# Loading the first rows in two column blocks, one transfer for batch 1 and the rest of the first queries, and a rewritten end of the token loop

## The chip, the core and the metric

The kernel runs on one NeuronCore of one Trainium2 chip. The metric is the device time of one execution in microseconds (us); less is better. Three runs of the kernel before took 171.71 to 171.78 us, median 171.75 us. TensorE (PE) multiplies, VectorE (DVE), ScalarE (ACT) and GpSimd (POOL) work on elements, and SyncE (SP) issues nearly all transfers, which 16 DMA engines carry out.

## The reference, cut to what matters

Linear attention over 8 batches of 8 heads, 576 tokens and 64 channels, an RMS norm per head, and then a soft mixture of experts over all 4608 tokens with 32 slots, four for each of eight experts:

```
kv  = einsum('bhsd,bhse->bhde', k, v)
out = einsum('bhsd,bhde->bhse', q, kv)
x   = out / sqrt(mean(out*out, -1) + 1e-6) * g_norm      # -> (4608, 512)
logits = x @ phi                                          # (4608, 32)
d = exp(logits - logits.max(0)); d /= d.sum(0)            # over tokens
slot_input = d.T @ x                                      # 32 slots x 512
slot_out[e] = relu(slot_input[e] @ w1[e]) @ w2[e]         # 8 experts
c = exp(logits - logits.max(1)); c /= c.sum(1)            # over slots
result = c @ slot_out                                     # (4608, 512)
```

All of it is float32. q, k and v are 28.3 MB together, the expert weights 33.6 MB, the result 9.4 MB.

## The kernel before, in words

The 4608 tokens are 36 tiles of 128. The program is written as one list of operations in the order of the Python code; each engine executes its own operations in that order, and `Order.emit` adds a semaphore wait wherever an operand was last written or read by another engine or by a transfer.

Start. SP issues five loads without any wait: `first_in` (phi, the norm's weights and the first half of batch 0's k and v, 9792 bytes a row, 128 rows), `kv0_in` (the rest of batch 0 and half of the first queries), `kv_in[0]` (batch 1's k and v), `q0_in` (the rest of the first queries) and `kv2_in`. TensorE meanwhile multiplies constants (`fill`, `fill_wide`), then forms batch 0's kv matrices in two halves. Later loads go into one arena in SBUF whose places are used again: each waits for the last reader of its place, mostly a matmul.

Token loop. For each tile T, `products(T)` makes one PSUM tile with the attention output and the unscaled logits per head, ACT squares it (`square`) and copies it out (`evict`). Two tiles are a stage: DVE sums the squares (`mean_square`), ACT makes the root by Ln and Exp (`root`), DVE improves it (`newton`), POOL scales (`scale_part`, `scale_x`), DVE adds the heads (`logits`). `kv_step(b, i)` forms the next batch's kv matrices; for batch 1 this stands ahead of tile 3's products. Six tiles are a group: `group_max` takes the running maximum of the logits, `group_max_T` and `group_max_row` bring it to all slots, `group_diag` and `group_exp_PE` broadcast it, `group_exp` takes exponentials and `group_sum` accumulates the slot inputs.

End of the loop (tiles A = 34 and Z = 35). Each of the two is a stage by itself (`STAGES` ends in 1, 1): root, newton, scaling of the logit part (`scale_o`, straight from PSUM), then `logits`, first for A, then for Z. Then `group_max` over the last six tiles, four small matmuls, the row maximum, `group_diag`, a matmul, `group_exp`, `scale_o` of the attention outputs, `group_sum`.

Experts and output. `expert_h(e)` needs w1 and the slot inputs, `expert_y(e, half)` needs w2; both weights stream through the arena, each load behind the last reader of its place. `gather` and `mix` bring the expert outputs to all partitions, `output` makes chunks of the result that go out in stores from SP (a few from POOL); the last store holds a third of the result.

Of the kernel before, what the change touches and what calls it, by code (L numbers as in the profile page):

```python
# [61 lines left out]
SHARED = (5, 11)  # L62
BEHIND = {4: (2, 3), 5: (4, 5, 6, 7)}
HEAD = 144
SCRATCH = 1024
WORK = {
    "kvT": (1, 256), "sq": (2, 1024), "part": (3, 512), "ms": (3, 16), "r0": (2, 16), "r": (3, 16), "r1": (2, 16),
    "top": (1, 128), "diag": (1, 32), "d": (2, 192), "alpha": (2, 1), "cm": (2, 13), "cs": (2, 13),
}
EPS_RMS = 1e-6  # L70
EPS_SUM = 1e-9
# [214 lines left out]
        at += n * size  # L286


def soft_moe_linear_attention(nc, first_in, kv0_in, kv_in, q0_in, kv2_in, kv4_in, kv5_in, t3_in, w_in, out):


    const = Const(nc)
# [12 lines left out]
    def load_row(at, src):  # L305
        nc.sync.dma_start(place(at, src.shape[-1]), src)
# [85 lines left out]
    def pos(T):  # L392
        return T + T // GROUPS[0] + 1
# [115 lines left out]
        nc.scalar.copy(xts[T % NX][:, :, :128], o[:, :, 32:160])  # L509


    def mean_square(s):
        mss[s] = wk.tile([P, STAGES[s] * H], F32, tag="ms", name=f"ms{s}", bufs=3)
        nc.vector.tensor_reduce(
            out=mss[s], in_=sqs.pop(s).rearrange("p t j (w d) -> p (t j w) d", w=2), axis=AX.X, op=ALU.add
        )

    def root(s, home=None):
# [26 lines left out]
                op=ALU.mult,  # L545
            )

    def scale_o(T, o, of_x):

        s = stage_of[T]  # L550
        r = rs_of[s][:, T - starts[s]].rearrange("p (j w) -> p j w", w=2).unsqueeze(3)
        if of_x:
            out = xts[T % NX][:, :, :128].rearrange("p j (w d) -> p j w d", w=2)
            src = o[:, :, 32:160].rearrange("p j (w d) -> p j w d", w=2)
        else:
            parts[s] = wk.tile([P, STAGES[s], H, NS], F32, tag="part", name=f"part{s}", bufs=3)
            out = parts[s][:, T - starts[s]].rearrange("p (j w) n -> p j w n", w=2)
            src = o[:, :, :192].rearrange("p j (c n) -> p j c n", n=NS)[:, :, 0::5]
        nc.vector.tensor_tensor(out=out, in0=src, in1=r.to_broadcast([P, 4, 2, D if of_x else NS]), op=ALU.mult)

    def scale_part(s, engine):
        part = parts[s]
        engine.tensor_tensor(
            out=part, in0=part, in1=rs_of[s].unsqueeze(3).to_broadcast([P, STAGES[s], H, NS]), op=ALU.mult
        )
# [15 lines left out]
        )  # L581


    ds, alphas, held, sums, pbs, pms, tops = {}, {}, {}, {}, {}, {}, {}
    g0 = [sum(GROUPS[:G]) for G in range(len(GROUPS) + 1)]

    def group_max(G):
        at = pos(g0[G])
        nc.vector.tensor_reduce(
            out=L[:, at + GROUPS[G]],  # L590
            in_=L[:, at - (G > 0) : at + GROUPS[G]].rearrange("p t n -> p n t"),
            axis=AX.X,
            op=ALU.max,
        )
        if G < len(GROUPS) - 1:
            tops[G] = wk.tile([P, 4, NS], F32, tag="top", name=f"top{G}", bufs=1)
            nc.vector.tensor_copy(
                out=tops[G], in_=L[:, at + GROUPS[G]].unsqueeze(1).to_broadcast([P, 4, NS])
            )

    def group_max_T(G):
        pm = ps.tile([P, P], F32, tag="m", name=f"pm{G}")
        if G in tops:
            nc.tensor.transpose(pm, tops.pop(G).rearrange("p a n -> p (a n)"), ident)
        for j in range(4 if G == len(GROUPS) - 1 else 0):
            nc.tensor.matmul(
                pm[32 * j : 32 * j + 32], lhsT=L[:, pos(g0[G]) + GROUPS[G]], rhs=ident, start=True, stop=True
            )
        pms[G] = pm

    def group_max_row(G):
        nc.vector.tensor_reduce(out=run_max[G % 2], in_=pms.pop(G), axis=AX.X, op=ALU.max)

    def group_diag(G):
        diag = wk.tile([P, NS], F32, tag="diag", name=f"diag{G}", bufs=1)
        nc.scalar.activation(diag, ident[:, :NS], AF.Copy, scale=run_max[G % 2])
        held[G] = diag

    def group_exp_PE(G):
        pbs[G] = ps.tile([P, NS], F32, tag="m", name=f"pb{G}")  # L620
# [94 lines left out]
    for g in range(2):  # L715
# [7 lines left out]
    load_row(KV_AT[3], kv_in[1])  # L723
    load_row(Q_AT[1] + 8, kv4_in)
    load_row(Q_AT[2], kv5_in)
    T_at, diag_at, pb_at, d_at, sums_at = {}, {}, {}, {}, {}
    for T in range(NT - 2):
        for b in range(1, B):
            for at in kv_steps.get((b, T - first[b]), ()):
                kv_step(b, at)  # L730
        late = [b for b in (1, 2) if T == first[b] - 1]
        o = products(T, (lambda: kv_step(late[0], 2)) if late else None)
        s = ends.get(T - 1)
        if s is not None:
            root(s)
        if T in diag_at:
            group_diag(diag_at[T])
        square(T, o)
        G = d_at.get(T)
        if G is not None:  # L740
            group_exp(G)
            sums_at[T + 1] = G
        evict(T, o)
        if T in T_at:
            group_max_T(T_at[T])
            diag_at[T + 1] = pb_at[T + 2] = T_at[T]
# [24 lines left out]
    tail_ps = ps.tile([P, 2, 512], F32, tag="kv", name="tail")  # L771
    A, Z = NT - 2, NT - 1
    oA = products(A)
    group_diag(G - 1)
    group_exp_PE(G - 1)
    root(s - 2)
    square(A, oA)
    newton(s - 2)
    scale_part(s - 2, nc.gpsimd)
    logits_adds(s - 2)  # L780
    scale_x(s - 2)
# [19 lines left out]
    fill_wide(ps.tile([P, 512], F32, tag="m", name="fill"), LATE_FILL[0])  # L801
    group_max_T(G)
    group_max_row(G)
    group_diag(G)
    scale_o(A, oA, True)
    fill(LATE_FILL[1], home=tail_ps[:, 1], cols=512)
    group_exp_PE(G)
    group_exp(G)
    scale_o(Z, oZ, True)
    fill(LATE_FILL[2], home=tail_ps[:, 1], cols=512)  # L810
    for i in range(0, GROUPS[G], 2):
        group_sum(G, i)
    fill(LATE_FILL[3], home=tail_ps[:, 1], cols=512)


    sTe = wk.tile([P, NE * 4 * NS], F32, tag="sq", name="sTe")
# [9 lines left out]
    fill(LATE_FILL[4], home=tail_ps[:, 1], cols=512)  # L826
    mine = psT[:, :P].rearrange("p (j e k) -> p e j k", j=4, k=SPE)
    last = NE - 1
    nc.vector.tensor_scalar_mul(
# [196 lines left out]
def build_program():  # L1026
    import concourse.bacc as bacc

    nc = bacc.Bacc("TRN2", target_bir_lowering=False, num_devices=1, dynamic_dma_scratch_size=SCRATCH)
    shapes = {  # L1030
        "first": (P, HEAD + 2304), "kv0": (P, 2304 + 2048), "kv": (2, P, TOK), "q0": (P, 2560),
        "kv2": (P, TOK + 2048),
        "kv4": (P, 2560 + TOK), "kv5": (P, 2 * TOK), "t3": (P, 3 * TOK),
        "w": (1, 2 * NE * P * UNIT),
    }
# [68 lines left out]
```

## Time and profile before

| | |
|---|---|
| median of three runs | 171.75 us |
| profiled execution: its time, its span | 171.73 us, 170.4 us |
| PE, DVE, ACT, POOL busy | 151.0, 86.9, 88.5, 59.6 us |
| moved by the DMA engines | 71.65 MB, mean 421 GB/s |
| time of the packets of SP's queue, as a share of 16 engines' span | 97.8% |

The span runs from the first to the last instruction; 1.3 us of the execution's time lie around it. In windows and slices, a DMA share of 1.00 means that the packets of that stretch fill all 16 engines; a packet is counted where it starts, so short stretches can show more than 1. "Idle before" in square brackets is the time that the engine stood idle ahead of a group, with what ended it.

### The profile page before, as it was taken

The page shows a single profiled execution, that of the slowest core. Times are in us where ns is not written, and L with a number is a line of the kernel's source. Part 1 is how long each engine was busy: PE and PEld are TensorE (multiplying, and loading weights), DVE is VectorE, ACT ScalarE, POOL GpSimd, SP SyncE. Part 2 cuts the span into 40 slices and gives each one's busy share as a digit, 9 for nine tenths or more (in the row PEclk, how much of TensorE's full clock was granted, in tenths as well). Part 3 has the DMA queues.
Part 4 walks back from the last instruction along what each step waited for, and adds up shares of the span by engine and source line. Part 5 has one row for each costly group of instructions (what it writes and reads, how often), then busy time and mean ns, then how long its engine had stood idle before and what let it go on. Part 6 is the DMA issues. An engine that isn't in the chain of part 4 may idle for free.

```text
span 170.4 us, 4234 instructions
## 1 busy us (share of the span) xinstructions
PE 151.0 (89%) x1834; PEld 104.0 (61%) x1834; DVE 86.9 (51%) x185; ACT 88.5 (52%) x230; POOL 59.6 (35%) x73
## 2 busy tenths in 40 slices
PE   7998998999999899999899989989999989989200
PEld 3457987979688888796696664345566533454000
DVE  1111437743677265763936798724888036319300
ACT  3015778786965887768849864202234044418300
POOL 7000247757356755366482589300000004000000
PEclk9999999999999999999999999999999999999855
DMA  5999999999999999999999999999999999999996
GB/s 193 440 435 417 478 413 409 457 430 478 419 415 439 432 441 413 419 400 460 400 458 408 448 408 423 431 458 396 431 427 431 452 435 396 427 415 439 415 447 288
DMA packets 3933, 71.65 MB, mean 421 GB/s; under 512 B 742, under 2 KB 742, under 8 KB 874
## 3 DMA queue, kind: packets, MB, share of 16 engines
q1 hardware_dynamic: 3562, 71.18, 97.8%
q8 instruction: 14, 0.23, 0.5%
q0 software_dynamic: 352, 0.20, 0.4%
q14 instruction: 5, 0.04, 0.1%
HBM read 61.94 MB, written 9.44 MB: 419 GB/s over the span
## 4 chain that ended last, share of the span: by engine, by line
PE 54%; DMA 16%; ACT 15%; DVE 6%; issue 1%; SPq 0%
PE psum L215 54%; DMA arena<-in_w_dram 10%; DMA arena<-in_kv_dram 6%; ACT bd L215 4%; ACT sq L215 4%; ACT xall L215 2%; DVE ms L215 2%; DVE logits L215 1%; ACT part L215 1%; ACT arena L215 1%; ACT r L215 1%; ACT d L215 1%; DVE part L215 1%; DVE acc L215 1%; DVE r L215 0%
## 5 line engine op out<-in xcount | busy, mean ns | idle before, releaser
L215 PE MATMUL psum<-bd,arena 128*128 128x192 f32 (+1 forms) x320 | 56.6, 336 | 2.4 <-ACT bd L215 1.2
L215 PEld LDWEIGHTS psum<-bd,arena 128*128 128x128 f32 (+1 forms) x320 | 45.5, 179 | 9.7 <-ACT xall L215 3.5
L215 DVE TENSOR_REDUCE ms<-sq 128x16 f32<-128x1024 f32 (+1 forms) x19 | 22.1, 1162 | 28.6 <-ACT sq L215 28.5
L215 POOL TENSOR_TENSOR part<-part,r 128x512 f32<-128x512 f32 x17 | 17.8, 1047 | 48.9 <-DVE r L215 48.9
L215 POOL TENSOR_TENSOR xall<-xall,r 128x512 f32<-128x512 f32 x34 | 34.7, 1042 | 0.0
L215 ACT ACTIVATE sq<-psum 128x512 f32<-128x512 f32 x36 | 21.5, 596 | 9.0 <-PE psum L215 8.9
L215 PEld LDWEIGHTS psum<-arena 128*64 128x64 f32 (+1 forms) x640 | 18.8, 137 | 6.6 <-issue 3.0
L215 PE MATMUL psum<-arena 128*64 128x64 f32 (+1 forms) x640 | 21.4, 226 | 0.3 <-DMA arena<-in_kv_dram 0.3
L215 ACT COPY xall<-psum 128x512 f32<-128x512 f32 x34 | 20.7, 608 | 0.0
L215 ACT COPY part<-psum 128x256 f32<-128x256 f32 (+1 forms) x38 | 13.7, 359 | 9.2 <-DVE part L215 8.0
L215 DVE TENSOR_REDUCE logits<-part 128x64 f32<-128x512 f32 (+1 forms) x18 | 17.8, 991 | 0.0
L215 PE MATMUL psum<-arena,xall 128*32 128x256 f32 x256 | 15.0, 380 | 0.4 <-DMA arena<-in_w_dram 0.4
L215 DVE COPY arena<-psum 128x768 f32<-128x768 f32 (+1 forms) x12 | 10.5, 889 | 6.8 <-PE psum L215 6.8
L215 ACT COPY arena<-psum 128x768 f32<-128x768 f32 (+1 forms) x14 | 10.2, 754 | 7.1 <-PE psum L215 7.1
L215 PE MATMUL psum<-logits,part 32*128 32x384 f32 x96 | 12.7, 527 | 0.6 <-ACT arena L215 0.4
L215 POOL DMA_DIRECT2D out_dram<-arena x2 | 1.2, 589 | 33.8 <-DVE arena L215 33.8
L215 PE MATMUL psum<-arena,sq 128*32 128x256 f32 x224 | 12.7, 379 | 0.2 <-DVE sq L215 0.2
L215 PEld LDWEIGHTS psum<-arena,xall 128*32 128x32 f32 x256 | 8.1, 110 | 6.9 <-issue 1.4
L215 PE MATMUL psum<-xall,d 128*32 128x258 f32 x144 | 10.8, 390 | 1.0 <-ACT d L215 1.0
L215 ACT COPY bd<-psum 64x128 f32<-64x128 f32 (+1 forms) x32 | 9.8, 308 | 2.4 <-PE psum L215 2.2
L215 PEld LDWEIGHTS psum<-arena,sq 128*32 128x32 f32 x224 | 7.2, 110 | 5.1 <-DVE sq L215 0.5
L215 ACT COPY kvT<-psum 128x256 f32<-128x256 f32 (+1 forms) x9 | 3.1, 348 | 12.6 <-PE psum L215 12.5
(80 smaller groups left out, 129.7 us busy)
## 6 DMA issues: line engine op xcount, KB each, us to landing
arena<-in_w_dram SPq DMA_DIRECT2D x4, 4096.0 KB, 23.8
arena<-in_w_dram SPq DMA_DIRECT2D x4, 2048.0 KB, 20.5
arena<-in_t_dram SPq DMA_DIRECT2D x1, 6912.0 KB, 35.6
arena<-in_w_dram SPq DMA_DIRECT2D x2, 3072.0 KB, 22.9
arena<-in_kv_dram SPq DMA_DIRECT2D x2, 2304.0 KB, 19.0
arena<-in_kv_dram SPq DMA_DIRECT2D x1, 4608.0 KB, 40.3
arena<-in_kv_dram SPq DMA_DIRECT2D x1, 3584.0 KB, 29.9
arena<-in_kv_dram SPq DMA_DIRECT2D x1, 3328.0 KB, 26.0
```

What stands on the lines that cost most here:

```text
L215: inst = getattr(engine, method)(*args, **kwargs)
```

## The change

Four edits.

1. The load of `first_in` is two loads: its first 512 columns (2048 bytes a row) and its other 1936 columns (7744 bytes a row).
2. `q0_in` and `kv_in[0]` are one load, `kv1_in`, 28672 bytes a row. The two parts are neighbours in the arena. The number of loads and the bytes stay as they were.
3. Tiles 34 and 35 are one stage. Both products stand next to each other; one root, one newton and one `logits` serve both. The last group's maximum is taken in steps: over its first two tiles early (`group_max(G, 2)`), the rest by three small operations (`last_max`). ACT scales tile A's attention output in eight pieces (`x_of_o`). There are 7 constant fills where there were 12.
4. `group_diag` and the matmul on it are replaced, in every group, by one transpose of the maximum's broadcast column.

```diff
-STAGES = (2,) * 17 + (1, 1)
+STAGES = (2,) * 18
-LATE_FILL = (4, 3, 3, 1, 1)
+LATE_FILL = (2, 1, 1, 1, 1, 1)
+AHEAD = 512
-    nc.sync.dma_start(arena[:, : HEAD + 2304], first_in)
+    nc.sync.dma_start(arena[:, :AHEAD], first_in)
+    nc.sync.dma_start(arena[:, AHEAD : HEAD + 2304], second_in)
     load_row(KV_AT[0] + 9, kv0_in)
-    load_row(KV_AT[1], kv_in[0])
-    load_row(Q_AT[0] + 8, q0_in)
+    load_row(Q_AT[0] + 8, kv1_in)
     load_row(KV_AT[2], kv2_in)
...
+    def last_max(G):
+        at = pos(g0[G])
+        so_far = L[:, at + GROUPS[G]]
+        m = wk.tile([P, 2, NS], F32, tag="kvT", name="last_max")
+        nc.vector.tensor_tensor(out=m, in0=L[:, at + 2 : at + 4], in1=L[:, at + 4 : at + 6], op=ALU.max)
+        nc.vector.tensor_tensor(out=so_far, in0=so_far, in1=m[:, 0], op=ALU.max)
+        group_top(G, so_far, m[:, 1])
...
-    def group_diag(G):
-        diag = wk.tile([P, NS], F32, tag="diag", name=f"diag{G}", bufs=1)
-        nc.scalar.activation(diag, ident[:, :NS], AF.Copy, scale=run_max[G % 2])
-        held[G] = diag
     def group_exp_PE(G):
-        nc.tensor.matmul(pbs[G], lhsT=ones, rhs=held[G], start=True, stop=True)
+        nc.tensor.transpose(pb, run_max[G % 2].to_broadcast([P, P]), ident)
...
-    mean_square(s - 1)
-    oZ = products(Z)
-    root(s - 1, tail_ps[:, 0, 256 : 256 + H])
-    square(Z, oZ)
-    newton(s - 1)
-    scale_o(A, oA, False)
-    mean_square(s)
-    root(s, tail_ps[:, 0, 256 + H : 256 + 2 * H])
-    logits(s - 1)
+    mean_square(s, slice(0, 1))
+    oZ = products(Z)
+    square(Z, oZ)
+    fill_wide(tail_ps[:, 1], LATE_FILL[0])
+    mean_square(s, slice(1, 2))
+    root(s, tail_ps[:, 0, 256 : 256 + 2 * H])
+    group_exp(G - 1)
+    todo_sums += [(G - 1, i) for i in range(0, GROUPS[G - 1], 2)]
+    group_max(G, 2)
     newton(s)
-    scale_o(Z, oZ, False)
+    scale_o(A, oA)
+    scale_o(Z, oZ)
+    x_of_o(A, oA, True)
     logits(s)
-    group_max(G)
+    last_max(G)
```

On SP, the first five loads of the kernel before and of the changed kernel, with partitions and columns of four bytes:

```order
L215 DMA arena<-in_first_dram 128x2448
L215 DMA arena<-in_kv_dram 128x4352
L215 DMA arena<-in_kv_dram 128x4608
L215 DMA arena<-in_q_dram 128x2560
L215 DMA arena<-in_kv_dram 128x6656
```

```order
L216 DMA arena<-in_first_dram 128x512
L216 DMA arena<-in_second_dram 128x1936
L216 DMA arena<-in_kv_dram 128x4352
L216 DMA arena<-in_kv_dram 128x7168
L216 DMA arena<-in_kv_dram 128x6656
```

Batch 1's k and v were the third load and end now with the fourth; everything from the fifth load on is the same.

On TensorE, ahead of tile 3: the last products of tile 2 (`psum<-bd,arena`), then batch 1's kv matrices (`psum<-arena`), which wait for a load (`dma_2` is batch 1's load before, `dma_3` the second part of the first queries before and the joint load now), then tile 3, and with `64x192` tile 4; before, then now:

```order
L215 MATMUL psum<-bd,arena 128x192 x3
L215 MATMUL psum<-arena 64x64 [waits dma_2]
L215 MATMUL psum<-arena 64x64 x39
L215 MATMUL psum<-bd,arena 128x192 [waits done_scalar]
L215 MATMUL psum<-bd,arena 128x192
L215 MATMUL psum<-ident,kvT 128x128 [waits done_scalar]
L215 MATMUL psum<-ident,kvT 128x128
L215 MATMUL psum<-gphi,kvT 128x128 x2
L215 MATMUL psum<-bd,arena 128x192 x2
L215 MATMUL psum<-bd,arena 64x192 [waits dma_3]
```

```order
L216 MATMUL psum<-bd,arena 128x192 x3
L216 MATMUL psum<-arena 64x64 [waits dma_3]
L216 MATMUL psum<-arena 64x64 x39
L216 MATMUL psum<-bd,arena 128x192 [waits done_scalar]
L216 MATMUL psum<-bd,arena 128x192
L216 MATMUL psum<-ident,kvT 128x128 [waits done_scalar]
L216 MATMUL psum<-ident,kvT 128x128
L216 MATMUL psum<-gphi,kvT 128x128 x2
L216 MATMUL psum<-bd,arena 128x192 x2
L216 MATMUL psum<-bd,arena 64x192
```

The wait for the second part of the first queries has moved ahead, from tile 4 to batch 1's kv matrices before tile 3.

On DVE, the end of the token loop, from the mean squares of tile 34 to the last row maximum (`small<-psum`); before, then now:

```order
L215 SCALAR_TENSOR_TENSOR r<-ms,psum 128x8 [waits done_scalar]
L215 SCALAR_TENSOR_TENSOR r<-r,psum 128x8 [waits done_vector] x2
L215 TENSOR_TENSOR part<-psum,r 128x256 [waits done_vector]
L215 TENSOR_REDUCE ms<-sq 128x8 [waits done_scalar]
L215 TENSOR_REDUCE logits<-part 128x32 [waits done_vector]
L215 SCALAR_TENSOR_TENSOR r<-ms,psum 128x8 [waits done_scalar]
L215 SCALAR_TENSOR_TENSOR r<-r,psum 128x8 [waits done_vector]
L215 SCALAR_TENSOR_TENSOR r<-r,psum 128x8 [waits done_gpsimd,done_vector]
L215 TENSOR_TENSOR part<-psum,r 128x256 [waits done_vector]
L215 TENSOR_REDUCE logits<-part 128x32 [waits done_vector]
L215 TENSOR_REDUCE logits<-logits 128x32 [waits done_gpsimd,done_vector]
L215 SCALAR_TENSOR_TENSOR acc<-acc,alpha,psum 128x258 [waits done_tensor]
```

```order
L216 TENSOR_REDUCE ms<-sq 128x8 [waits done_scalar] x2
L216 TENSOR_TENSOR d<-logits,psum 128x192
L216 TENSOR_REDUCE logits<-logits 128x32
L216 SCALAR_TENSOR_TENSOR r<-ms,psum 128x16 [waits done_scalar]
L216 SCALAR_TENSOR_TENSOR r<-r,psum 128x16 [waits done_vector] x2
L216 TENSOR_TENSOR part<-psum,r 128x256 [waits done_vector]
L216 TENSOR_TENSOR part<-psum,r 128x256
L216 TENSOR_REDUCE logits<-part 128x64 [waits done_vector]
L216 TENSOR_TENSOR kvT<-logits 128x64 [waits done_gpsimd,done_vector]
L216 TENSOR_TENSOR logits<-logits,kvT 128x32 [waits done_vector]
L216 TENSOR_TENSOR top<-logits,kvT 128x128 [waits done_vector]
L216 SCALAR_TENSOR_TENSOR acc<-acc,alpha,psum 128x258 [waits done_scalar,done_tensor]
```

One chain through both tiles stands where two stood, and the previous group's exponent argument (`d<-logits,psum`) has moved behind the second mean square.

## Rows read from the trace of the kernel before

**Rows 1.** Page, DMA in 40 slices, busy tenths
```profile
DMA  5999999999999999999999999999999999999996
```

**Rows 2.** Windows: stretch, length, busy per engine, PEclk, DMA share, GB/s
```profile
0.00:2.00 2.00, 0.94 (x3) 0.39 (x4) 0.73 (x3) 1.26 (x1) 0.91 (x9) 1.00 0.31 49
2.00:4.00 2.00, 2.00 (x5) 0.85 (x4) 0.00 (x0) 0.02 (x1) 2.00 (x6) 1.00 0.75 299
4.00:6.00 2.00, 2.00 (x4) 0.66 (x2) 0.00 (x0) 0.00 (x0) 0.10 (x1) 1.00 1.05 444
...
160.00:162.00 2.00, 0.00 (x0) 0.00 (x0) 0.00 (x0) 0.00 (x0) 0.00 (x0) 0.64 1.05 449
162.00:169.00 7.00, 0.00 (x0) 0.00 (x0) 0.00 (x0) 0.00 (x0) 0.00 (x0) 0.50 1.01 434
169.00:170.40 1.40, 0.00 (x0) 0.00 (x0) 0.00 (x0) 0.00 (x0) 0.00 (x0) 0.50 0.05 18
```

**Rows 3.** Timeline of SP: start, us, what it issued
```profile
0.74 0.38 SPq L215 DMA_DIRECT2D arena<-in_first_dram  x1
1.18 0.89 SPq L215 DMA_DIRECT2D arena<-in_kv_dram  x2
2.12 0.64 SPq L215 DMA_DIRECT2D arena<-in_q_dram  x1
...
159.42 0.33 SPq L215 DMA_DIRECT2D out_dram<-arena  x1
```

**Rows 4.** DMA issues of single stretches: count, KB, us from issue to landing
```profile
arena<-in_first_dram SPq DMA_DIRECT2D x1, 1224.0 KB, 5.3
arena<-in_q_dram SPq DMA_DIRECT2D x1, 1280.0 KB, 18.8
out_dram<-arena SPq DMA_DIRECT2D x1, 3072.0 KB, 10.9
```

**Rows 5.** Timeline of PE: start, us, what, idle before
```profile
18.48 2.48 PE L215 MATMUL psum<-arena 128*64 128x64 f32 x80
109.98 1.52 PE L215 MATMUL psum<-xall,d 128*32 128x258 f32 x24 [0.19 <-ACT d L215]
128.93 5.36 PE L215 MATMUL psum<-arena,xall 128*32 128x256 f32 x96
134.70 1.67 PE L215 MATMUL psum<-arena,xall 128*32 128x256 f32 x25 [0.41 <-DMA arena<-in_w_dram]
157.84 0.92 PE L215 MATMUL psum<-logits,part 32*128 32x384 f32 x4 [0.20 <-ACT arena L215]
```

**Rows 6.** Timeline, end of the token loop: PE, ACT and DVE
```profile
100.08 1.55 PE L215 MATMUL psum<-bd,arena 128*128 128x192 f32 x8
97.70 0.33 PE L215 MATMUL psum<-ident,top 128*128 128x128 f32 x1
103.00 0.59 ACT L215 ACTIVATE sq<-psum 128x512 f32<-128x512 f32 x1
109.56 0.36 ACT L215 ACTIVATE d<-d 128x192 f32<-128x192 f32 x1 [0.89 <-DVE d L215]
104.05 0.67 DVE L215 TENSOR_REDUCE ms<-sq 128x8 f32<-128x512 f32 x1
105.45 0.36 DVE L215 SCALAR_TENSOR_TENSOR r<-r,psum 128x8 f32<-128x8 f32 x2
105.85 0.42 DVE L215 TENSOR_TENSOR part<-psum,r 128x256 f32<-128x256 f32 x1
99.59 1.04 DVE L215 TENSOR_REDUCE logits<-part 128x64 f32<-128x512 f32 x1
106.94 0.54 DVE L215 TENSOR_REDUCE logits<-logits 128x32 f32<-128x224 f32 x1
108.03 0.29 DVE L215 TENSOR_REDUCE small<-psum 128x1 f32<-128x128 f32 x1 [0.16 <-PE psum L215]
109.17 0.35 DVE L215 TENSOR_TENSOR d<-logits,psum 128x192 f32<-128x192 f32 x1 [0.26 <-PE psum L215]
```

More of the change, by code (lines that the diff above doesn't have):

```diff
@@ L286, in first_pieces, with soft_moe_linear_attention @@
         at += n * size
-def soft_moe_linear_attention(nc, first_in, kv0_in, kv_in, q0_in, kv2_in, kv4_in, kv5_in, t3_in, w_in, out):
+def soft_moe_linear_attention(nc, first_in, second_in, kv0_in, kv1_in, kv2_in, kv3_in, kv4_in, kv5_in, t3_in, w_in, out):
     const = Const(nc)
@@ L509, in evict, with mean_square @@
         nc.scalar.copy(xts[T % NX][:, :, :128], o[:, :, 32:160])
-    def mean_square(s):
-        mss[s] = wk.tile([P, STAGES[s] * H], F32, tag="ms", name=f"ms{s}", bufs=3)
+    def mean_square(s, tiles=slice(0, 2)):
+        if s not in mss:
+            mss[s] = wk.tile([P, STAGES[s] * H], F32, tag="ms", name=f"ms{s}", bufs=3)
         nc.vector.tensor_reduce(
-            out=mss[s], in_=sqs.pop(s).rearrange("p t j (w d) -> p (t j w) d", w=2), axis=AX.X, op=ALU.add
+            out=mss[s][:, tiles.start * H : tiles.stop * H],
+            in_=sqs[s][:, tiles].rearrange("p t j (w d) -> p (t j w) d", w=2),
+            axis=AX.X,
+            op=ALU.add,
         )
@@ L546, in scale_x, with scale_o, x_of_o @@
             )
[L548 to L554, printed above, removed]
-        else:
[L556 to L559, printed above, removed]
+    def scale_o(T, o):
+        s, i = stage_of[T], T - starts[stage_of[T]]
+        if i == 0:
+            parts[s] = wk.tile([P, STAGES[s], H, NS], F32, tag="part", name=f"part{s}", bufs=3)
+        r = rs_of[s][:, i].rearrange("p (j w) -> p j w", w=2).unsqueeze(3).to_broadcast([P, 4, 2, NS])
+        out = parts[s][:, i].rearrange("p (j w) n -> p j w n", w=2)
+        src = o[:, :, :192].rearrange("p j (c n) -> p j c n", n=NS)[:, :, 0::5]
+        nc.vector.tensor_tensor(out=out, in0=src, in1=r, op=ALU.mult)
+    def x_of_o(T, o, by_head):
+        r = rs_of[stage_of[T]][:, T - starts[stage_of[T]]]
+        x = xts[T % NX]
+        if by_head:
+            for h in range(H):
+                at = h % 2 * D
+                nc.scalar.activation(
+                    x[:, h // 2, at : at + D], o[:, h // 2, 32 + at : 32 + at + D], AF.Copy, scale=r[:, h : h + 1]
+                )
+        else:
+            nc.vector.tensor_tensor(
+                out=x[:, :, :128].rearrange("p j (w d) -> p j w d", w=2),
+                in0=o[:, :, 32:160].rearrange("p j (w d) -> p j w d", w=2),
+                in1=r.rearrange("p (j w) -> p j w", w=2).unsqueeze(3).to_broadcast([P, 4, 2, D]),
+                op=ALU.mult,
+            )
     def scale_part(s, engine):
@@ L581, in logits, with group_max @@
         )
-    ds, alphas, held, sums, pbs, pms, tops = {}, {}, {}, {}, {}, {}, {}
+    ds, alphas, sums, pbs, pms, tops = {}, {}, {}, {}, {}, {}
     g0 = [sum(GROUPS[:G]) for G in range(len(GROUPS) + 1)]
-    def group_max(G):
+    def group_max(G, n=None):
         at = pos(g0[G])
@@ L594, in group_max, with four, group_top @@
         )
[L595 to L599, printed above, removed]
+        if n is None:
+            group_top(G, L[:, at + GROUPS[G]])
+    def four(a):
+        return a.unsqueeze(1).to_broadcast([P, 4, NS])
+    def group_top(G, a, b=None):
+        tops[G] = wk.tile([P, 4, NS], F32, tag="top", name=f"top{G}", bufs=1)
+        if b is None:
+            nc.vector.tensor_copy(out=tops[G], in_=four(a))
+        else:
+            nc.vector.tensor_tensor(out=tops[G], in0=four(a), in1=four(b), op=ALU.max)
+    def last_max(G):
[5 more added lines that the diff above has]
+        group_top(G, so_far, m[:, 1])
     def group_max_T(G):
         pm = ps.tile([P, P], F32, tag="m", name=f"pm{G}")
[L603 to L608, printed above, removed]
+        nc.tensor.transpose(pm, tops.pop(G).rearrange("p a n -> p (a n)"), ident)
         pms[G] = pm
@@ L773, in soft_moe_linear_attention @@
     oA = products(A)
-    group_diag(G - 1)
     group_exp_PE(G - 1)
-    root(s - 2)
+    root(s - 1)
     square(A, oA)
[L778 to L781, printed above, removed]
+    newton(s - 1)
+    scale_part(s - 1, nc.gpsimd)
+    logits_adds(s - 1)
+    scale_x(s - 1)
+    mean_square(s, slice(0, 1))
[4 more added lines that the diff above has]
+    root(s, tail_ps[:, 0, 256 : 256 + 2 * H])
     group_exp(G - 1)
     todo_sums += [(G - 1, i) for i in range(0, GROUPS[G - 1], 2)]
-    mean_square(s - 1)
-    oZ = products(Z)
-    root(s - 1, tail_ps[:, 0, 256 : 256 + H])
-    square(Z, oZ)
-    newton(s - 1)
-    scale_o(A, oA, False)
-    mean_square(s)
-    root(s, tail_ps[:, 0, 256 + H : 256 + 2 * H])
-    logits(s - 1)
+    group_max(G, 2)
     newton(s)
-    scale_o(Z, oZ, False)
+    scale_o(A, oA)
+    scale_o(Z, oZ)
+    x_of_o(A, oA, True)
     logits(s)
-    group_max(G)
+    last_max(G)
     for i in todo_sums:
@@ L1030, in build_program @@
     shapes = {
-        "first": (P, HEAD + 2304), "kv0": (P, 2304 + 2048), "kv": (2, P, TOK), "q0": (P, 2560),
-        "kv2": (P, TOK + 2048),
+        "first": (P, AHEAD), "second": (P, HEAD + 2304 - AHEAD), "kv0": (P, 2304 + 2048), "kv1": (P, 2560 + TOK),
+        "kv2": (P, TOK + 2048), "kv3": (P, TOK),
         "kv4": (P, 2560 + TOK), "kv5": (P, 2 * TOK), "t3": (P, 3 * TOK),
```

38 lines of the change are left out of this document (18 added, 20 removed).

## The prediction

> **What bounds the kernel now.** I read the slices first, then the windows at both ends, then what SP issues and when it lands, and last the engines' timelines where the change acts. The slices show DMA at nine tenths or more in all 40 but the first and the last, at a mean of 421 GB/s [rows 1]. PE is busy 89% too, and the chain of waits runs mostly over PE, so the page alone could be read as a PE kernel. The ends decide. PE's last matmul ends at 157.84 + 0.92 = 158.76 us and the last store is issued at 159.42, but the store lands 10.9 us later, at 170.3, the end of the span [rows 3 to 5]. Between these the DMA engines run at a share of 1.01 to 1.05 and 434 to 449 GB/s [rows 2]: they carry out what was queued. Loads and stores are one stream without a hole, and the end is the start of that stream, plus its bytes at some 430 GB/s, plus a taper: after 169 us hardly a packet starts [rows 2]. Time on PE, ACT or DVE counts only if it makes the stream run dry.
>
> How near is that? The last store is 3072 KB, 3.15 MB. Counted back from the end by the windows, 25 KB start after 169.0 and 3.04 MB between 162 and 169, so its first packets start at about 161.8, which is 2.4 us after its issue. At the start of the kernel, issue at 0.74 led to ten packets before 2.00 (49 GB/s over 2 us), so an idle queue needs at most 1.26 us [rows 2, 3]. The last store may thus be issued about 1.1 us later before any engine waits for it. Ahead of that PE itself waited 0.41 us for a w2 load at 134.70 [rows 5]. Compute in the token loop can be late by 0.4 + 1.1 = 1.5 us before the end moves; being early gains nothing.
>
> **The first load in two blocks.** The bytes and the number of transfers in the stream do not change, as the split adds one and the join of batch 1 with the rest of the first queries takes one away. What can change is how the stream starts. Between 2 and 4 us it moves 299 GB/s at a share of 0.75, and 444 GB/s right after [rows 2]: 2 x (444 - 299) = 290 KB are missing, 0.65 us of stream. That is all there is to win. At the other end the second block could come too late: SP's issues are 0.89 / 2 = 0.44 us apart [rows 3], and if the first block's 256 KB were gone before the second is there, the stream could stand for up to 0.44 us. At 444 GB/s 256 KB last 0.59 us, longer than 0.44, so I give this little weight. In between: an engine moves 444 / 16 = 27.8 GB/s, so a row of 9792 bytes takes it 0.35 us and one of 2048 bytes 0.07. If an engine gets up to speed with the end of its first row, small first rows bring this forward by 0.28 us; if the slow start is a latency that does not ask for the row's length, by nothing. I take 0.28 us, near the middle of 0 and 0.65, as an estimate.
>
> The Trainium skill, "DMA: Bandwidth & Descriptors" (Rules for kernel authors), speaks against this edit: it asks for at least 1 MiB per DMA, and the first block has a quarter of that. Its Anatomy of one DMA puts a fixed cost of about 2.0 us on each; were it paid in the stream, the split would cost 2.0 us and the join give it back, a sum of nothing, and no window here shows such a pause between transfers.
>
> **Batch 1 and the rest of the first queries in one transfer.** Batch 1's kv matrices start on PE at 18.48 us with no idle time for a load noted ahead of them [rows 5]. Now they wait for the join, whose last byte has the same place in the stream as the last byte of the first queries, issued at 2.12 and landed 18.8 us later, at 20.92 [rows 3, 4]. PE stands for 20.92 - 18.48 = 2.44 us, or 2.16 with the stream 0.28 us ahead. Behind the waiting matmuls stand tile 3 and all that follows; ACT, DVE and POOL drain and wait, and from tile 3 on the loop is the same chain of PE, ACT and DVE as before, so I let the whole delay carry to the end of the loop. Loads that wait for PE are issued as much later; the DMA share that never drops in mid-kernel says that work was queued ahead of each of them [rows 1], though not how much.
>
> **The end of the token loop.** Before, the last sums over tokens begin at 109.98 [rows 5], with two chains of root, newton, scale and head sum one behind the other. Now there is one, which begins when tile 35's products end, 100.08 + 1.55 = 101.63. By [rows 6]: square 0.59, mean square 0.67; then, beside ACT's root, DVE's exponent argument of the group before 0.35 and the early maximum, at most 0.54; newton, three operations at 0.18, 0.54; scale 0.42 for each tile, 0.84; head sum over both 1.04; three small maxima, not shown before, taken at 0.35 each as the larger neighbour (0.2 to 0.35), 1.05; transpose 0.33, row maximum 0.29, transpose 0.33, exponent argument 0.35, exponential 0.36. Sum 7.28, so 108.9. Handovers add some hundredths each, and DVE operations that follow each other overlap by as much as a tenth; so 108.3 to 109.2, a gain of 0.8 to 1.7 us, and I take 1.2. Tile A's scaling in eight pieces on ACT fits behind newton, and the sums of the group before, now released about 1.5 us later, lie on PE while DVE is on this chain.
>
> **The diag edit.** One ACT operation less per group and a matmul for a matmul. ACT does not set the end; I cost it at nothing.
>
> **Sum.** The loop ends 2.16 - 1.2 = about 1.0 us later (0.5 to 1.6). PE's wait at 134.70 takes 0.4 of it and the last store is issued near 160.0, with 0.5 us of cover left. So compute costs nothing, and the stream's start gives 0.28 us: 171.73 (profiled execution) - 0.28 = 171.45 us. The median of the runs before is 171.75, the same within 0.02.
>
> **Rivals.**
> 1. The start is latency that does not depend on the row: nothing at the start, compute still covered, 171.7 us. For it: PE's and SP's work at the start is the same, and all engines start from an idle queue. Against it: the share between 2 and 4 us is 0.75, not 0, so something rises there that could depend on size.
> 2. The end moves because the loop is too late. This turns on one wait, PE's 2.2 to 2.4 us for the joint load. After the last matmul, at 158.76, the granted clock's mean over 160 to 162 is 0.64 and then 0.50 [rows 2, 5], so it fell from 2.4 to 1.2 GHz at 160.6, 1.8 us after PE stopped. PE's new wait is longer than that. If the clock falls there, batch 1's matmuls (2.48) and the tiles behind (1.55 each) run slower, up to double; with 2.0 us more the loop is 3.0 us late, 1.5 beyond the 1.5 of cover, and the time is 171.45 + 1.5 = 172.95. It decides from 1.5 us of delay on. Against it: how much quieter PE must be in mid-loop than at the end no row shows, and engines that finish early at the taper have slack of their own. The Trainium skill, "TensorE: Matmul & The Clock Gate" (HAM oscillation), describes just this, waits for DMA between bursts of matmuls that bring the lower clock back.
> 3. The second block is late for the first: 171.73 + 0.44 = 172.2.
> 4. The whole rise goes away: 171.73 - 0.65 = 171.1.
>
> **Chances and range.** A measurement of this kernel can tell 0.2%, 0.34 us. The forecast, a gain of 0.1 to 0.6 us around 0.28, has 0.58, of which I give 0.35 to gains beyond 0.34 us; rival 1 has 0.18, rival 2 0.13 (0.02 of it too small to tell), rival 3 0.07, rival 4 0.04. Faster 0.35 + 0.04 = 0.39, same 0.23 + 0.18 + 0.02 = 0.43, slower 0.11 + 0.07 = 0.18. The range of 8 in 10 reaches from rival 4's 171.1 to rival 3's 172.2; most of rival 2 lies beyond it. The forecast's own range is 171.15 to 171.65.
>
> **What would show it.** Right: the rate between 2 and 4 us rises well above 299 GB/s; PE stands ahead of batch 1's kv matrices until about 20.6; the sums over the last group start about 1 us later than 109.98; PE's wait of 0.41 us at the w2 load is gone; the last store is issued near 160.0 and the DMA share stays at 1.0 to 169 us. Wrong: a hole in the DMA share after 160 us or a granted clock below 1.00 near 21 us (rival 2), a rate of about 299 GB/s as before (rival 1) or lower (rival 3).

## The result, and the profile after

The changed kernel takes 172.91 us in the median of 8 runs (172.22 to 173.90), the kernel before 171.70 on the same chip: ratio 1.0069, 95% interval 1.0044 to 1.0094. It is slower by 1.2 us, and it spreads over 1.7 us where the kernel before spreads over 0.4. The forecast was 171.45. The profiled execution took 172.76 us, with a span of 171.4.

Both ends of the changed kernel in windows, as in [rows 2] (stretch, length, busy per engine, granted clock, DMA share, GB/s):

```profile
0.00:2.00 2.00, 0.94 (x3) 0.40 (x4) 0.73 (x3) 1.27 (x1) 0.91 (x9) 1.00 0.04 4
2.00:4.00 2.00, 2.00 (x5) 0.86 (x4) 0.49 (x1) 0.02 (x1) 2.00 (x6) 1.00 0.93 355
4.00:6.00 2.00, 2.00 (x4) 0.67 (x2) 0.34 (x2) 0.00 (x0) 0.15 (x1) 1.00 1.07 450
...
160.00:162.00 2.00, 0.92 (x6) 0.30 (x4) 1.25 (x2) 1.33 (x3) 0.00 (x0) 1.00 0.98 418
162.00:169.00 7.00, 0.00 (x0) 0.00 (x0) 0.00 (x0) 0.00 (x0) 0.00 (x0) 0.58 1.00 430
169.00:170.40 1.40, 0.00 (x0) 0.00 (x0) 0.00 (x0) 0.00 (x0) 0.00 (x0) 0.50 0.74 316
```

Between 2 and 4 us the stream moves 355 GB/s instead of 299, but before 2 us it moves 4 instead of 49: (355 - 299) x 2 = 112 KB more and 90 KB less. The missing start has only moved. At the other end 316 GB/s still run after 169.0, where there were 18.

SP's timeline, as in [rows 3]; the third row holds three loads, the last one is the last store:

```profile
0.74 0.39 SPq L216 DMA_DIRECT2D arena<-in_first_dram  x1
1.19 0.42 SPq L216 DMA_DIRECT2D arena<-in_second_dram  x1
1.65 1.64 SPq L216 DMA_DIRECT2D arena<-in_kv_dram  x3
...
161.78 0.33 SPq L216 DMA_DIRECT2D out_dram<-arena  x1
```

The last store is issued 2.36 us later than at 159.42. The forecast had about 160.0. PE's timeline tells on the way where this comes from [rows 5]:

```profile
21.11 2.48 PE L216 MATMUL psum<-arena 128*64 128x64 f32 x80 [2.29 <-DMA arena<-in_kv_dram]
...
109.80 0.33 PE L216 MATMUL psum<-ident,top 128*128 128x128 f32 x1 [0.96 <-DVE top L216]
...
110.51 0.32 PE L216 MATMUL psum<-ident,small 128*128 128x128 f32 x1 [0.17 <-DVE small L216]
...
111.67 2.66 PE L216 MATMUL psum<-xall,d 128*32 128x258 f32 x24 [0.62 <-ACT d L216]
...
116.34 3.66 PE L216 MATMUL psum<-arena,sq 128*32 128x256 f32 x64 [0.19 <-DVE sq L216]
...
131.91 7.09 PE L216 MATMUL psum<-arena,xall 128*32 128x256 f32 x128
139.41 0.79 PE L216 MATMUL psum<-part,sel 128*128 128x128 f32 x4 [0.41 <-DVE part L216]
...
160.21 0.92 PE L216 MATMUL psum<-logits,part 32*128 32x384 f32 x4 [0.20 <-ACT arena L216]
```

Batch 1's kv matrices wait for the joint load, as forecast, and begin 2.63 us later than at 18.48. The last group's sums begin 1.69 us later than at 109.98, so the new end of the loop gives back about 0.9. But these sums take 2.66 us where they took 1.52. The 128 matmuls on w2 run through without the wait of 0.41 us. The next windows say why the sums are slow:

```profile
110.00:112.00 2.00, 1.21 (x12) 0.36 (x14) 1.39 (x4) 0.55 (x2) 0.67 (x1) 0.97 1.00 426
112.00:114.00 2.00, 2.00 (x24) 0.80 (x16) 0.00 (x0) 0.00 (x0) 0.00 (x0) 0.50 1.23 524
114.00:116.00 2.00, 1.95 (x12) 1.03 (x8) 0.53 (x2) 0.00 (x0) 0.00 (x0) 0.68 0.92 393
```

The granted clock (the third value from the end) is 0.50 from 112 to 114: PE has its lower level, 1.2 GHz, just where the chain runs over it alone. In the kernel before it is 1.00 up to 160. The first expert's matmuls (`psum<-arena,sq`) begin at 116.34, 2.98 us later than before (113.36).

What a late store does to the stream is seen near the end of the same trace:

```profile
157.00:158.00 1.00, 1.00 (x14) 0.70 (x10) 0.85 (x2) 0.69 (x2) 0.00 (x0) 1.00 0.90 387
159.00:160.00 1.00, 1.00 (x10) 0.37 (x6) 0.85 (x2) 0.69 (x2) 0.00 (x0) 1.00 0.89 375
161.00:162.00 1.00, 0.12 (x2) 0.00 (x0) 0.56 (x1) 0.48 (x1) 0.00 (x0) 1.00 0.95 406
```

Single windows of 1 us also fall below 0.95 in the kernel before, as a packet counts where it starts. Counted by bytes it is plain: the stream passes each number of bytes 0.37 us later than before by 130 us, 0.68 by 156, 0.82 by 160, 0.93 by 163. The first part grows evenly through the loop, the rest comes in steps ahead of the stores.

### The profile page after: what moved, and what is told of

Read it like the earlier page. It is cut to its first block, busy times and chain, and to the rows that moved or that the text cites. A ratio compares the mean times of both kernels' runs of the same rounds, so it can differ in the third digit from the quotient of the medians.

```text
span 171.4 us, 4195 instructions
## 1 busy us (share of the span) xinstructions
PE 149.6 (87%) x1815; PEld 102.9 (60%) x1815; DVE 86.8 (51%) x183; ACT 88.6 (52%) x230; POOL 59.7 (35%) x73
## 4 chain that ended last, share of the span: by engine, by line
PE 58%; ACT 14%; DMA 11%; DVE 9%; issue 1%; SPq 1%
PE psum L216 58%; DMA arena<-in_kv_dram 11%; ACT bd L216 4%; ACT sq L216 3%; DVE ms L216 3%; DVE logits L216 2%; ACT xall L216 2%; DVE part L216 1%; ACT part L216 1%; ACT arena L216 1%; ACT r L216 1%; SPq L216 1%; DVE r L216 1%; ACT d L216 1%; DVE acc L216 1%
## 5 line engine op out<-in xcount | busy, mean ns | idle before, releaser
L216 POOL TENSOR_TENSOR xall<-xall,r 128x512 f32<-128x512 f32 x34 | 34.8, 1044 | 0.0
L216 DVE TENSOR_REDUCE logits<-part 128x64 f32<-128x512 f32 x17 | 17.7, 1041 | 0.0
L216 PE MATMUL psum<-xall,d 128*32 128x258 f32 x144 | 11.9, 428 | 1.1 <-ACT d L216 1.1
```

The costliest lines, as they stand in the source:

```text
L216: inst = getattr(engine, method)(*args, **kwargs)
```

## The experiments

All were timed in alternation with the kernel before (171.66 to 171.75 in the median of each group). The rival causes: the late compute (theory 1), the lower clock at the end of the loop (2), the two-block start (3), the place of the tiles in SBUF, as the list of work tiles became shorter (4), the new operations themselves (5).

**The load edits one by one.** Three kernels: the changed kernel with batch 1 and the second queries apart again; the kernel before with the join alone; the kernel before with the two-block load alone.

```diff
-    load_row(Q_AT[0] + 8, kv1_in)      # e1_no_join; e2_join_only has it the other way round
+    load_row(KV_AT[1], kv1_in)
+    load_row(Q_AT[0] + 8, q0_in)
...
-    nc.sync.dma_start(arena[:, : HEAD + 2304], first_in)      # e3_split_only
+    nc.sync.dma_start(arena[:, :AHEAD], first_in)
+    nc.sync.dma_start(arena[:, AHEAD : HEAD + 2304], second_in)
```

> The changed kernel with batch 1 and the rest of the first queries in two transfers again, as before; the split start and the new end of the loop stay. Theory 1 (late compute: PE's 2.3 us wait for the join, less the 0.8 us that the new end of the loop gives back, is more than the stream's cover, and stores come late): PE's wait ahead of batch 1 is gone, the sums over the last group start near 109, 1 us before those of the kernel before, no hole in the DMA share after 155 us, time 171.4 to 171.8. Theory 2 (the lower clock at the end of the loop alone, from fewer constant fills): the granted clock falls near 110 us here too and the time stays above 172.2. Theory 3 (the split start itself costs, since the slowest engine ended the first load 0.28 us later): 172.0.

> The kernel before with the join alone. Theory 1: the loop is late by the whole 2.4 us, PE starts the output phase 2 us later than 134.7, the last store is issued near 161.4, a hole of about 0.9 us opens, 172.3 to 172.8. Theory 2: the old fills keep the clock at 1.00 through the end of the loop, so 171.7 unless it falls in the wait at 18 to 21 us. Theory 3: 171.7, since the start is the old one.

> The kernel before with the split of the first load alone. Forecast on record: 171.45 (the start gives 0.28 us). Theory 3: 171.9 to 172.0, as the holes of the stream at 2.8 to 3.1 and 5.2 to 5.5 us outweigh the quicker first rows. Theories 1 and 2 say nothing on the sign and allow 171.4 to 171.8.

Without the join: 172.40 us (172.36 to 172.50), ratio 1.0041 (1.0029 to 1.0053). The join alone: 172.82 (172.38 to 173.80), 1.0074 (1.0047 to 1.0101). The two blocks alone: 171.72, 1.0000 (0.9992 to 1.0009), with this start:

```profile
0.00:2.00 2.00, 0.94 (x3) 0.40 (x4) 0.73 (x3) 1.27 (x1) 0.91 (x9) 1.00 0.11 14
2.00:4.00 2.00, 2.00 (x5) 0.86 (x4) 0.42 (x1) 0.02 (x1) 2.00 (x6) 1.00 0.95 349
4.00:6.00 2.00, 2.00 (x4) 0.68 (x2) 0.34 (x2) 0.00 (x0) 0.14 (x1) 1.00 1.00 420
```

The split neither gains nor costs. The join costs by itself and brings the spread. But most of the median's loss stays without it, so a second cause lies in the rest.

That second cause is not the clock, although theory 2 seems to come out: in the profiled execution without the join the granted clock is 0.50 from 110 to 112 us, and the last sums take 2.79 us.

```profile
109.70 2.79 PE L216 MATMUL psum<-xall,d 128*32 128x258 f32 x24 [0.63 <-ACT d L216]
```

But this execution, at a mean clock of 0.960, took 172.40 us, and the four others, at 0.974 to 0.979, took 172.36 to 172.50. With the join it is different. Of the six executions of the join alone, the three at a mean clock of 0.975 to 0.978 took 172.38 to 172.44 us, the three at 0.966 to 0.970 took 173.19 to 173.80. The profiled one is of the first kind (172.38), at a granted clock of 1.00 from 18 to 26 and from 106 to 120 us:

```profile
21.03 2.48 PE L215 MATMUL psum<-arena 128*64 128x64 f32 x80 [2.41 <-DMA arena<-in_kv_dram]
```

```profile
161.23 0.33 SPq L215 DMA_DIRECT2D out_dram<-arena  x1
```

So the joint load costs about 0.7 us by its lateness, without any lower clock, and the spread above that goes with a lower mean clock.

**The rest of the change, and the place of the tiles.** The list of work tiles lost `diag` (32 columns), so everything behind it moved down by 128 bytes a row. Four kernels: the changed kernel without both load edits; the same with the old list; the kernel before with the new list (`diag` behind everything); the kernel before with the transpose in place of `diag`, nothing moved.

```diff
-    "top": (1, 128), "diag": (1, 32), "d": (2, 192), ...      # e6_new_layout; e5_old_layout the other way round
+    "part": (3, 512), "top": (1, 128), "ms": (3, 16), ...
...
+        pb = ps.tile([P, P], F32, tag="m", name=f"pb{G}")      # e7_transpose_only
+        nc.tensor.transpose(pb, run_max[G % 2].to_broadcast([P, P]), ident)
```

> The changed kernel with both edits of the loads undone: only the one stage for the last two tiles, the maximum in steps and the transpose in place of the diag. Theory 1: sums over the last group near 109.1, the stream has no hole, and earlier compute gains nothing: 171.7. Theory 2: the clock falls near 110 us in part of the runs; here compute is early enough to cover 1.2 us, so 171.7 to 172.0. Theory 3: 171.7.

> The run with only the new end of the loop and the transposes (172.25 us) again, but with the work tiles in SBUF at the places of the kernel before (the unused diag tile kept, the tile of the maximum back behind the others), so that everything allocated behind them has its old address. Theory 4 (place in SBUF: the changed list of work tiles moves the arena and all behind it by 128 bytes, and load packets of the token loop take some ns longer, 24576 bytes 915 instead of 912 ns on average): packets back at 912 ns, 171.65 to 171.8. Theory 5 (the new operations themselves, the broadcast transposes or the end of the loop, slow the stream): still 172.2.

> The kernel before with nothing changed but the list of work tiles in the changed kernel's order and size (the diag tile allocated behind everything else). Theory 4: load packets lengthen by some ns and the time is 172.1 to 172.3. Theory 5: 171.7.

> The kernel before with the transpose of the broadcast maximum in place of the diag and its matmul in every group; the diag tile stays allocated, so no address moves. Theory 4: 171.7. Theory 5, if the transposes are what slows the stream: 172.0 to 172.3, with packets of 24576 bytes at about 915 ns.

The rest alone: 172.25, ratio 1.0034 (1.0021 to 1.0047). With the old list: 172.02 (171.68 to 172.38), 1.0018 (1.0008 to 1.0028). The kernel before with nothing but the new list: 172.39 (172.30 to 172.42), 1.0042 (1.0029 to 1.0055). The transpose: 171.90, 1.0017 (1.0008 to 1.0026). The place alone costs 0.7 us. The trace of that kernel shows PE at its w2 load, and the last store:

```profile
132.72 1.91 PE L215 MATMUL psum<-arena,xall 128*32 128x256 f32 x32
135.52 1.72 PE L215 MATMUL psum<-arena,xall 128*32 128x256 f32 x28 [0.89 <-DMA arena<-in_w_dram]
```

```profile
160.27 0.33 SPq L215 DMA_DIRECT2D out_dram<-arena  x1
```

PE comes there 0.34 us later than before (134.63 instead of 134.29), but the load is later still: PE waits 0.89 us instead of 0.41 and starts 0.82 later [rows 5]. By bytes, the stream is late by 0.10 us at 30 us, 0.30 at 90 and 0.54 at 130, and by no more behind, where stores run: the loads run slower. A packet of 32768 bytes takes 1216 ns in the median instead of 1213, one of 16384 bytes 613 instead of 611. All packets together take 0.50 us more for each of the 16 engines, of which about 0.1 is not loads but instruction fetches (last section). Three more places, all in the kernel with the transpose:

```diff
-    "top": (1, 128), "diag": (1, 32), "d": (2, 192), "alpha": (2, 1), "cm": (2, 13), "cs": (2, 13),
+    "top": (1, 128), "diag": (1, 16), "d": (2, 192), ...      # e13_place_64; (1, 24) in e15_place_32
+    "top": (1, 128), "diag": (1, 32), "d": (2, 192), "alpha": (2, 1),      # e14_place_256; cm, cs behind the arena
```

> The kernel before with the transpose in place of the diagonal and its product (171.9 us by itself), and the small tile that is unused then cut from 32 to 16 columns, so that the arena and all behind it lie 64 bytes lower in each partition's row: blocks at byte 20160, a multiple of 64 and no more, where they were at 20224 (a multiple of 256) and in the changed kernel at 20096 (a multiple of 128). If what counts is the power of two of the place, packets are at least as long as in the changed kernel (1216 ns or more for 32768 bytes, 1213 before) and the time is 172.4 us or more. If only that one place is bad, 1213 ns and 171.9 us.

> The same kernel as the run before it, with the unused tile whole and the tiles cm and cs allocated behind the arena, so that the arena lies 256 bytes lower than before: blocks at byte 19968, a multiple of 512. If the place by its multiple counts, packets are as long as before or shorter (1213 ns or less for 32768 bytes) and the time is 171.9 us or less. If any move from the place before is bad, 1216 ns and 172.4 us.

> As the first run of this group, with the unused tile cut to 24 columns: 32 bytes lower than before, blocks at byte 20192, a multiple of 32 and no more. If the place by its multiple counts, the longest packets of the three, above 1216 ns, and the slowest, 172.5 us or more. If it does not, 171.9 us.

| the arena's blocks begin at a multiple of | kernel | packet of 32768, 16384 bytes, ns | time, us |
|---|---|---|---|
| 512 bytes | 256 lower | 1213, 611 | 171.76 |
| 256 | before, at its place | 1213, 611 | 171.70 |
| 128 | before, with the new list | 1216, 613 | 172.39 |
| 64 | 64 lower | 1215, 613 | 172.52 |
| 32 | 32 lower | 1216, 614 | 172.64 |

It is the place and not the move: 256 bytes lower costs nothing, 64 or 32 bytes lower cost 0.8 to 0.9 us. In these five places the step lies between multiples of 256 and of 128.

**How much lateness the stream takes.** Constant products on PE ahead of batch 1's kv matrices in the kernel before, five and two; nothing else differs.

```diff
+        if T == first[1] - 1:
+            fill_wide(ps.tile([P, 512], F32, tag="m", name="fill"), 5)      # 2 in e12_short_delay
```

> The kernel before with five constant matmuls of 512 columns (5 x 0.47 = 2.35 us) on TensorE ahead of batch 1's kv matrices: the delay of the join without an idle TensorE and without touching a transfer. Theory 1 (late compute beyond 1.5 us of cover opens a hole): the last store near 161.4, holes before 158 and 162 us, about 0.5 to 0.9 us, 172.2 to 172.6, steady from run to run. If the join alone (172.82, spread 1.4 us) loses by the lower clock after an idle TensorE: 171.7 to 172.2 here and a small spread.

> The kernel before with two constant products of 0.9 us each on PE ahead of batch 1's kv matrices: everything behind is about 1.8 us later, PE's wait of 0.41 us at 134.70 goes, gather about 1.3 us later than before. With a cover of 1.5 us behind that wait: 171.7 us, unchanged. If the stores ahead of the last one have less cover than the last (five such products cost 2.2 us), up to 172.2.

Five: 173.91 us, ratio 1.0132 (1.0118 to 1.0146), far above what was expected; two: 171.84, 1.0014 (1.0003 to 1.0025). Of the five, the trace shows PE's row, the last store, and two windows:

```profile
18.43 4.45 PE L215 MATMUL psum<-ones 128*128 128x512 f32 x10
```

```profile
163.06 0.33 SPq L215 DMA_DIRECT2D out_dram<-arena  x1
```

```profile
148.00:150.00 2.00, 2.00 (x40) 0.94 (x32) 1.23 (x2) 0.80 (x1) 0.00 (x0) 1.00 0.90 277
159.00:160.00 1.00, 1.00 (x10) 0.54 (x8) 0.96 (x2) 1.00 (x2) 0.00 (x0) 1.00 0.66 283
```

The five took 4.4 us and not the 2.35 that the expectation put in; the expectation's size was wrong, not the theory. Where stores come too late, the stream drops to 277 and 283 GB/s, and not only ahead of the last store.

**The clock.** The kernel before with the join, and two constant products in PE's wait; the changed kernel with an unused tile of 32 columns ahead of the work tiles, so that the arena lies as before; the same with two products in the wait and three constant products more at the end of the loop; and this without the join, and so without the wait and the products in it.

```diff
+    "pad": (1, 32), "kvT": (1, 256), ...      # e9_pad, e11_pad_filled, e16_pad_no_join
+            fill_wide(ps.tile([P, 512], F32, tag="m", name="fill"), 2)      # e10_join_filled, e11_pad_filled
-LATE_FILL = (2, 1, 1, 1, 1, 1)
+LATE_FILL = (2, 3, 1, 2, 1, 1)      # e11_pad_filled, e16_pad_no_join
```

> The kernel before with the join alone, and two constant matrix products (0.9 us each) on PE in the 2.4 us in which it waits for the joint load. If the wait is what brings the lower clock later in some executions of the join alone (172.4 to 173.8 us), the mean clock is 0.975 to 0.979 in all of them and the time is 172.4 us with little spread. If the spread has another cause, it stays: 172.4 to 173.8, median 172.8.

> The changed kernel with one unused tile of 32 columns (128 bytes a row) ahead of the work tiles, so that the arena and everything behind it lie where they lay in the kernel before. Lateness theory (the end comes when the last stores are late, by lateness less about 1.5 us of cover, or by the slower packets, whichever is more): PE's gather at 139.0, 2.4 us later than before, last store near 161.7, so 172.3 to 173.5 us, median about 172.7, still spread, and packets as short as before. Additive theory (the slower packets' 0.7 us come on top): 172.91 - 0.7 = 172.2 us. If the order of the work tiles and not the arena's place makes the packets longer, the packets stay 2 to 4 ns longer and the time is 172.9.

> The changed kernel with the unused tile of the first run of this group, two constant products in PE's wait for the joint load, and two wide and one short constant product more at the end of the token loop, so that neither stretch leaves PE idle for long. Lateness theory: the granted clock stays at 2.4 GHz to the end of the matmuls, the last group's sums take 1.52 us and not 2.66, PE's gather is 2.5 - 0.7 - 0.4 = 1.4 us later than before, within the cover: 171.7 us, as before. If the delay by the join costs by itself, 172.4. If the clock falls all the same, 172.5 to 173.

> The changed kernel without the join (batch 1's kv matrices and the rest of the first queries in two transfers again), with the arena at its old place and two wide and one short constant product more at the end of the loop. Lateness theory: no wait at 18.5 us, PE about 0.7 us ahead of the kernel before, clock at 2.4 GHz to the last matmul, stream as before: 171.7 us, the same as before (0.9992 to 1.0012 in the ratio), as being early gains nothing. If the new end of the loop gains by itself, 171.0 to 171.4; if it costs by itself, 172.2.

The filled join: 172.36 (172.17 to 172.52), ratio 1.0036 (1.0024 to 1.0048). The unused tile alone: 174.18 (172.51 to 174.79), 1.0122 (1.0085 to 1.0159). With the products: 172.32 (172.19 to 172.53), 1.0037 (1.0024 to 1.0050). Without the join as well: 171.77, 1.0000 (0.9990 to 1.0011). The unused tile alone shows what the products take away, PE's rows and windows:

```profile
21.29 3.91 PE L216 MATMUL psum<-arena 128*64 128x64 f32 x80 [2.48 <-DMA arena<-in_kv_dram]
...
113.29 2.81 PE L216 MATMUL psum<-xall,d 128*32 128x258 f32 x24 [0.63 <-ACT d L216]
```

```profile
163.40 0.33 SPq L216 DMA_DIRECT2D out_dram<-arena  x1
```

```profile
20.00:22.00 2.00, 0.71 (x14) 0.72 (x16) 0.17 (x1) 0.82 (x3) 1.71 (x2) 0.77 1.02 439
22.00:24.00 2.00, 2.00 (x42) 2.00 (x42) 0.00 (x0) 0.00 (x0) 1.34 (x2) 0.50 1.05 453
```

Here the clock fell during the wait for the joint load: batch 1's kv matrices take 3.91 us instead of 2.48. It fell again at the last sums (2.81 instead of 1.52), and the last store was issued at 163.40. The packets are as short as before (1213 ns), so the median's excess over the changed kernel is not the place; why the mean clock was low in all six of its runs (0.946 to 0.964), but only in five of the eight of the changed kernel (0.954 to 0.966, the others 0.972 to 0.980), is open. With the products both places keep the clock: the changed kernel with the unused tile has its last sums at 112.19 in 1.52 us, and in the filled join the wait is 0.65 us and the granted clock 1.00 in both stretches:

```profile
18.44 1.88 PE L215 MATMUL psum<-ones 128*128 128x512 f32 x4
20.97 2.48 PE L215 MATMUL psum<-arena 128*64 128x64 f32 x80 [0.65 <-DMA arena<-in_kv_dram]
...
112.41 1.52 PE L215 MATMUL psum<-xall,d 128*32 128x258 f32 x24 [0.19 <-ACT d L215]
```

```profile
112.19 1.52 PE L216 MATMUL psum<-xall,d 128*32 128x258 f32 x24 [0.41 <-ACT d L216]
```

The last line is the changed kernel's with the unused tile and the products. The kernels by the issue of their last store, and by their profiled executions against 171.73 us, with three more of these issues (two products; unused tile and products; filled join):

```profile
160.49 0.33 SPq L215 DMA_DIRECT2D out_dram<-arena  x1
...
161.00 0.33 SPq L216 DMA_DIRECT2D out_dram<-arena  x1
...
161.23 0.33 SPq L215 DMA_DIRECT2D out_dram<-arena  x1
```

| kernel | last store later by | time more by | difference |
|---|---|---|---|
| before, two products | 1.07 | 0.31 | 0.76 |
| changed, unused tile and products | 1.58 | 0.59 | 0.99 |
| join, filled | 1.81 | 0.62 | 1.19 |
| join alone | 1.81 | 0.65 | 1.16 |
| changed | 2.36 | 1.03 | 1.33 |
| before, five products | 3.64 | 2.40 | 1.24 |
| changed, unused tile | 3.98 | 2.63 | 1.35 |

Above 1.8 us of lateness each further microsecond costs about one, whatever made it; in these executions 0.3 to 0.6 us are paid before that, so the cover does not end at one point. The place's 0.7 us do not add to it, as the changed kernel's difference (1.33) is no smaller than that of kernels at the old place. A reason for this, which no run tests by itself: in the changed kernel the stream is 0.4 us late already, and a late stream needs its stores later.

Without the join, at the old place and with the constant products, the changed kernel equals the kernel before; with the join and two products in its wait it loses 0.6 us (172.32), and without the join, but at the new place and without the products, 0.7 (172.40). No kernel here is faster than the kernel before; a better version did not come out.

## Why the prediction was wrong

Two steps failed: the sum by which the loop ends about 1.0 us late and stays within the cover, and the diag edit at nothing. In the order of the forecast:

- **What bounds the kernel:** right. The stream sets the end, and compute counts only where the stream runs dry. Two products on PE ahead of batch 1's kv matrices moved the loop's end by 1.7 us and the median by 0.1.
- **The cover of 1.1 us behind the wait of 0.41:** right within 0.3, by the table's last column from 1.8 us of lateness on (1.2 to 1.35 us); below that some of the price is paid earlier. It was read at the last store alone; the stores ahead of it run short as well.
- **"I take 0.28 us" for the two blocks:** wrong, 0.00 us. Rival 1 had this: the wait for the first bytes does not depend on the row's length. The 256 KB still landed 2.7 us after their issue, and the rate of 355 GB/s that was to prove the gain was made up for by 4 GB/s ahead of it. The forecast's test looked at one window and should have summed two. The Trainium skill, "DMA: Bandwidth & Descriptors" (Anatomy of one DMA), gives the fixed cost of 2.0 us that the forecast quotes for transfers that GpSimd issues, while SP issues these; no run here shows it in the stream.
- **The joint load, "2.16 to 2.44 us":** right in mechanism, mis-sized: kv matrices 2.63 later, and 2.51 at tile 34's products (101.05 instead of 98.54), as no stream ahead by 0.28 shortened it.
- **The end of the loop, "I take 1.2":** 0.82 (2.51 - 1.69), the low end of its range. DVE's rows show the largest single excess:

```profile
106.59 0.76 DVE L216 TENSOR_TENSOR part<-psum,r 128x256 f32<-128x256 f32 x2
107.38 1.07 DVE L216 TENSOR_REDUCE logits<-part 128x64 f32<-128x512 f32 x1
108.49 0.70 DVE L216 TENSOR_TENSOR kvT<-logits 128x64 f32<-128x64 f32 x1
109.22 0.19 DVE L216 TENSOR_TENSOR logits<-logits,kvT 128x32 f32<-128x32 f32 x1
```

  The first small maximum took 0.70 us, not 0.35, the second only 0.19. The chain from the last product (104.03) to the sums took 7.64 instead of 7.28, with the other terms some tenths longer or shorter.
- **"The loop ends about 1.0 us later ... last store near 160.0":** this step failed. Late at the sums 1.69, at the first expert 2.98: 1.29 us were lost in between, while the granted clock was 0.50. Less 0.60 taken up behind, 0.41 of it by PE's wait, 2.4 us remain where 0.6 were forecast. The profiled execution is 1.03 us longer, so 1.33 us of this were covered. In the end of the loop alone the same fall cost nothing to be seen: without both load edits three executions at a mean clock of 0.959 or 0.960 took 172.25 to 172.38 us, the two at 0.975 and 0.979 took 172.19 and 172.25. The fall cost time where the join had used up the cover.

  The forecast took the wait for the joint load as the only place for the lower clock (rival 2, 0.13, 172.95 us). That place is real, as the unused tile's run shows. But the 1.8 us from the kernel's end settle nothing about it: after waits of 2.29 us (the changed kernel) and 2.41 (the join alone) the granted clock stayed at 1.00, and in the wait of 2.48 of the unused tile's run it fell. In the changed kernel's profiled execution the clock fell at the other thin stretch, the end of the loop, where the change had also taken 5 of 12 constant products away (three put back there, and the sums take 1.52 us again) and PE waits 0.96, 0.17 and 0.62 us between small matmuls. Rival 2's time came out; its place was half right. The Trainium skill, "TensorE: Matmul & The Clock Gate" (HAM oscillation), describes such a wait, one for transfers between bursts of matmuls that brings the lower clock; the trace of the unused tile's kernel agrees, with 3.91 us for work of 2.48 right behind a wait of 2.48, at a granted clock of 0.50.
- **"The diag edit. I cost it at nothing":** wrong by a way that the forecast never looked at. The operations are close to nothing (171.90 with the transpose alone, of which 0.2 us is not explained), but the tile that went moved the arena off a multiple of 256 bytes, which costs 0.7 us by itself. The two runs of the changed kernel with a mean clock of 0.98 took 172.22 and 172.42, like the kernel before with the new list (172.39). So without a fall of the clock the change loses 0.5 to 0.7 us, and either the place or the lateness by the join is enough for that.
- **The range** ended at 172.2, as rival 2 was given 0.13.

Why the kernels with the old list and the transpose spread up to 172.4 is open. In the profiled execution of one of them (172.37 us) a single DMA engine ended 0.5 us behind all others, with the mean of the 16 only 0.2 later than before.

## What to carry to other kernels

Where a stream of transfers sets the end, work out the cover in front of every store and sum all lateness up to it, the lower clock behind each new thin stretch of PE included: a wait and a row of small matmuls are both such stretches, and constant products in them are worth their place. Before a work tile is removed or resized, look where the tiles behind it come to lie, and put a spare tile in if the transfers' targets lose their multiple of 256 bytes. A window that gains at the start proves nothing until the window ahead of it is added.

## What the hardware showed unexpectedly

- Loads into places that are multiples of 128, 64 or 32 bytes take up to 5 ns more in the median for a packet of 16 to 55 KB than at multiples of 256 or 512; by 130 us the stream is 0.4 to 0.7 us late. The stores out of the same places are not slower (912 ns for 24576 bytes in all of them).
- In these same kernels the 14 packets of 16384 bytes that the profile lists as instruction fetches, and that no load of the program issues, take 1044 to 1066 ns in the mean instead of 926 to 945. The cause is open.
- The clock falls in some executions of one program and not in others: in two of eight runs of the changed kernel the mean clock (0.98) has no room for a fall, and the time is 172.22 and 172.42 instead of up to 173.90. One more, at 0.972, took 173.18; whether the clock fell there the mean does not tell.
